# Loading Q of a grouped-query attention kernel: sixteen DMA transposes, or eight plain loads and transposes on TensorE

## Chip, cores and metric

The kernel runs on one core of a Trainium2 chip. The metric is the device time of one execution in microseconds (us), as the median of several runs. A profiled execution ("the profile", "the trace") gives spans; its span is 1.8 us shorter than the measured time where the record gives both for one execution.

## The reference

```python
B, Hq, Hkv, Sq, Sk, D = 16, 32, 8, 16, 2048, 128        # all bf16
k = jnp.repeat(k, 4, axis=1); v = jnp.repeat(v, 4, axis=1)
scores = jnp.einsum("bhqd,bhkd->bhqk", q, k) * D ** -0.5
out    = jnp.einsum("bhqk,bhkd->bhqd", jax.nn.softmax(scores, axis=-1), v)
```

The four query heads of a key head have 4 x 16 = 64 query rows, so there are 128 groups of 64 rows, and the kernel takes them two at a time: 64 **pairs** of 128 rows. K and V are 64 MiB each; Q and the output are 2 MiB each. Each pair needs 2 MiB of K and V.

## The kernel before

For each pair the work is: transpose both groups' K on TensorE into PSUM and evict it (KT), multiply Q by it (S), take the row maximum on VectorE (`max`), exponentiate on ScalarE (`exp`), transpose the probabilities on TensorE and evict them (PT), multiply by V (PV), normalise (`norm`) and store. Q lies transposed in SBUF, as `QT[d, row]`, and is the stationary operand of S.

A 128x1024 half tile of KT or PT passes through one of only three staging banks of PSUM. VectorE or ScalarE evicts it. A bank must have been evicted before the third half tile after it can be transposed.

The order of the operations on each engine is fixed when the kernel is built. A generator, `build_schedule`, plays a list-scheduling model with assumed durations and DMA rates and writes down the order in which things start. Its times are assumptions, but the order it chose is then binding: in the traces before the change TensorE ran its 5,632 instructions in exactly the generated order.

```python
_DUR = {"KT_load": 0.46, "PT_load": 0.46, "S": 0.75, "PV": 1.02, ...
        ("act", "kte"): 1.07, ("act", "pte"): 1.07, ("act", "exp"): 2.08, ..., "Q": 3.3}
_SIZE = {"K": 0.5, "V": 0.5, "Q": 0.25 * 1.45, "ST": 0.03125 * 1.45}
QCH = 512            # rows of Q per load: one load serves four pairs
...
sched = build_schedule(NP, pairs_per_qch)
pe_prog, dve_prog, act_prog, sp_prog = sched["pe"], sched["dve"], sched["act"], sched["sp"]
...
def issue_q(c):      # SyncE: one of sixteen DMA transposes of 512 rows
    sp.dma_start_transpose(QT[:, qch * c:qch * (c + 1)], qf[qch * c:qch * (c + 1), :]).then_inc(sem_q[c], 16)
...
# TensorE, transposes of K: one staging bank per half
pe.wait_ge(sem_k[s], 16 * (g // NBK + 1))
for ld in lds:
    wait_bank_free(ld)
    for t in range(8):
        ins = pe.transpose(stage_ap(ld["bank"], t), Kn[s][:, 8 * ld["half"] + t, :], ident[:, :])
    ins.then_inc(sem_stage, 1)
...
# TensorE, score product: QT is the stationary operand
ins = pe.matmul(S_ps[64 * gg:64 * (gg + 1), 512 * c:512 * (c + 1)],
                QT[:, 128 * p + 64 * gg:128 * p + 64 * (gg + 1)],
                kt[:, gg, 4 * c:4 * (c + 1), :], start=True, stop=True)
...
# ScalarE, eviction (VectorE has the same with tensor_copy)
act.wait_ge(sem_stage, ld["u"] + 1)
act.activation(evac_dst(ld), stage_bank_ap(ld["bank"]), ACT.Copy).then_inc(sem_ev["act"], 1)
```

SyncE issues all DMAs in order: K two tiles per pair, V three pairs later, the store seven pairs later. There are 12 buffers for K and 16 for V.

Of the kernel before, what the change touches and what calls it, by code (L numbers as in the profile page):

```python
# [16 lines left out]
NSTAGE = 3  # L17
DV = 3
DSTORE = 7
QCH = 512  # L20
QLEAD = 6


_DUR = {
    "KT_load": 0.46, "PT_load": 0.46, "S": 0.75, "PV": 1.02,
    ("dve", "kte"): 0.63, ("dve", "pte"): 0.63, ("dve", "max"): 2.30, ("dve", "recip"): 0.17, ("dve", "norm"): 0.36,
    ("act", "kte"): 1.07, ("act", "pte"): 1.07, ("act", "exp"): 2.08, ("act", "norm"): 0.46,
    "K": 0.65, "V": 0.65, "ST": 0.65, "Q": 3.3,
}
_LAT = 0.12  # L30
_LAT_SAME = 0.04
# [1 line left out]
_BW = 0.371  # L33
_BW_SLOW = 0.364
_RING_MB = 5.2
_SIZE = {"K": 0.5, "V": 0.5, "Q": 0.25 * 1.45, "ST": 0.03125 * 1.45}
_T0 = 7.0


# [20 lines left out]
def build_schedule(NP, qch_pairs, nbk=NBK, nbv=NBV, nbo=NBO, nkt=NKT, npt=NPT, nstage=NSTAGE, opts=None):  # L60
# [6 lines left out]
    def t(key):  # L67
        return done.get(key, INF)

    pe_left = []  # L70
    for p in range(NP):
        pe_left += [("KT", p, 0), ("KT", p, 1), ("S", p), ("PT", p), ("PV", p)]
    x_left = []
    for p in range(NP):
        x_left += [("kte", p, gg, h) for gg in range(2) for h in range(2)]
        x_left += [("pte", p, h) for h in range(2)]
        x_left += [("max", p), ("recip", p), ("exp", p), ("norm", p)]
# [12 lines left out]
    def eng_options(op):  # L90
        k = op[0]
        if k in ("max", "recip"):
            return ("dve",)
        if k == "exp":
            return ("act",)
        if k == "kte":
            return opts["kte_engs"]
        if k == "pte":
            return opts["pte_engs"]
        return opts["norm_engs"]  # L100

    def ready_pe(op):
        kind = op[0]
        r = []
        if kind == "KT":
            p, gg = op[1], op[2]
            r.append(t(("dma", "K", 2 * p + gg)))
            if p >= nkt and ("S", p - nkt) not in pe_sched:
                return INF
            u0 = next_u[0]  # L110
            for h in range(2):
                if u0 + h >= nstage:
                    r.append(t(("evac", u0 + h - nstage)))
        elif kind == "S":
            p = op[1]
            r.append(t(("dma", "Q", p // qch_pairs)))
            for gg in range(2):
                for hh in range(2):
                    key = ("KT", p, gg, hh)
                    if key not in load_u:  # L120
                        return INF
                    r.append(t(("evac", load_u[key])))
            if p >= 1:
                r.append(t(("max", p - 1)))
        elif kind == "PT":
            p = op[1]
            r.append(t(("exp", p)))
            if p >= npt and ("PV", p - npt) not in pe_sched:
                return INF
            u0 = next_u[0]  # L130
            for h in range(2):
                if u0 + h >= nstage:
                    r.append(t(("evac", u0 + h - nstage)))
        elif kind == "PV":
            p = op[1]
            for hh in range(2):
                key = ("PT", p, None, hh)
                if key not in load_u:
                    return INF
                r.append(t(("evac", load_u[key])))  # L140
            for gg in range(2):
                r.append(t(("dma", "V", 2 * p + gg)))
            if p >= 1:
                r.append(t(("norm", p - 1)))
        return max(r) if r else 0.0

    def ready_x(op):
        kind = op[0]
        r = []
        if kind == "kte":  # L150
            key = ("KT", op[1], op[2], op[3])
            if key not in load_u:
                return INF
            r.append(t(("load", load_u[key])))
        elif kind == "pte":
            key = ("PT", op[1], None, op[2])
            if key not in load_u:
                return INF
            r.append(t(("load", load_u[key])))
        elif kind == "max":  # L160
            p = op[1]
            r.append(t(("S", p)))
            if p >= 2:
                r.append(t(("exp", p - 2)))
        elif kind == "recip":
            r.append(t(("exp", op[1])))
        elif kind == "exp":
            p = op[1]
            r.append(t(("max", p)))
            if p >= 2:  # L170
                r.append(t(("PT", p - 2)))
        elif kind == "norm":
            p = op[1]
            r += [t(("PV", p)), t(("recip", p))]
            if p >= nbo:
                r.append(t(("dma", "ST", p - nbo)))
        return max(r) if r else 0.0
# [10 lines left out]
    def ready_sp(op):  # L188
        kind, x = op
        r = [ring_ok_time(_SIZE[kind])]  # L190
        if kind == "K":
            if x >= nbk:
                r.append(t(("KT", (x - nbk) // 2, (x - nbk) % 2)))
        elif kind == "V":
            if x >= nbv:
                r.append(t(("PV", (x - nbv) // 2)))
        elif kind == "ST":
            r.append(t(("norm", x)))
        return max(r) if r else 0.0

    KIND_PRIO = {"S": 0, "max": 0, "exp": 0, "PT": 1, "pte": 1, "PV": 2, "recip": 2, "norm": 2, "KT": 3, "kte": 3}

    while pe_left or x_left or sp_left:
        best = None
# [7 lines left out]
        for op in pe_left:  # L212
            rd = ready_pe(op)
            if rd == INF:
                continue
            st = max(free["pe"] + _LAT_SAME, rd + _LAT)
            cand = ((round(st, 3), op[1], KIND_PRIO[op[0]]), st, "pe", op)
            if best is None or cand[0] < best[0]:
                best = cand
            seen += 1  # L220
            if seen > 12:
                break
        seen = 0
        for op in x_left:
# [7 lines left out]
                engs = (fin[0][1],)  # L232
            for eng in engs:
                st = max(free[eng] + _LAT_SAME, rd + _LAT)
                cand = ((round(st, 3), op[1], KIND_PRIO[op[0]]), st, eng, op)
                if best is None or cand[0] < best[0]:
                    best = cand
            seen += 1
# [17 lines left out]
        elif eng == "pe":  # L256
            pe_left.remove(op)
            pe_sched.add(op)
            if kind in ("KT", "PT"):
                en = st  # L260
                for h in range(2):
                    uu = next_u[0]
# [11 lines left out]
        else:  # L274
            x_left.remove(op)
            en = st + DUR[(eng, kind)]
            if kind == "kte":
                done[("evac", load_u[("KT", op[1], op[2], op[3])])] = en
            elif kind == "pte":
                done[("evac", load_u[("PT", op[1], None, op[2])])] = en  # L280
            else:
                done[(kind, op[1])] = en
# [7 lines left out]
def bass_standalone__gqa_softmax__sampling_kernel(  # L290
# [27 lines left out]
    ident = sb("ident", [128, 128], BF16)  # L318
    iota_t = sb("iota_t", [128, 128], I32)
    QT = sb("QT", [128, NROWS], BF16)  # L320
    Kn = [sb(f"Kn{i}", [128, J, 128], BF16) for i in range(NBK)]
    Vb = [sb(f"Vb{i}", [128, J, 128], BF16) for i in range(NBV)]
    KT = [sb(f"KT{i}", [128, 2, J, 128], BF16) for i in range(NKT)]
# [29 lines left out]
    loads = []  # L353
    kt_loads = {}
    pt_loads = {}
    for op in pe_prog:
        if op[0] == "KT":
            _, p, gg = op
            for h in range(2):
                ld = dict(kind="KT", pair=p, gg=gg, half=h, u=len(loads), eng=None, eidx=None)  # L360
# [9 lines left out]
                pt_loads[(p, h)] = ld  # L370

    def op_load(op):
        if op[0] == "kte":
            return kt_loads[(op[1], op[2], op[3])]
        if op[0] == "pte":
            return pt_loads[(op[1], op[2])]
        return None
# [49 lines left out]
    with nc.Block() as block:  # L427
# [7 lines left out]
        @block.sync  # L435
        def _(sp):
            def issue_q(c):
                sp.dma_start_transpose(QT[:, qch * c:qch * (c + 1)], qf[qch * c:qch * (c + 1), :]).then_inc(sem_q[c], 16)

            def issue_k(g):  # L440
                s = g % NBK
# [38 lines left out]
        def _(pe):  # L480
# [6 lines left out]
                    pe.wait_ge(sem_ev[prev["eng"]], prev["eidx"])  # L487

            for op in pe_prog:
                if op[0] == "KT":  # L490
                    _, p, gg = op
                    lds = [kt_loads[(p, gg, h)] for h in range(2)]
                    g = grp(p, gg)
# [8 lines left out]
                        ins.then_inc(sem_stage, 1)  # L502
                elif op[0] == "S":
                    _, p = op
                    pe.wait_ge(sem_q[(128 * p) // qch], 16)
                    for sm, n in evac_waits([kt_loads[(p, gg, h)] for gg in range(2) for h in range(2)]):
                        pe.wait_ge(sm, n)
                    if p >= 1:
                        pe.wait_ge(sem_max, p)
# [21 lines left out]
                elif op[0] == "PV":  # L531
# [18 lines left out]
                            )  # L550
                    ins.then_inc(sem_pv, 1)

        def evac_dst(ld):
            p, h = ld["pair"], ld["half"]
            if ld["kind"] == "KT":
                return KT[p % NKT][:, ld["gg"], 8 * h:8 * (h + 1), :]
            return PT[p % NPT][:, 8 * h:8 * (h + 1), :]

        @block.vector
        def _(dve):  # L560
            for op in dve_prog:
                ld = op_load(op)
                if ld is not None:
                    dve.wait_ge(sem_stage, ld["u"] + 1)
                    dve.tensor_copy(evac_dst(ld), stage_bank_ap(ld["bank"])).then_inc(sem_ev["dve"], 1)  # L565
                elif op[0] == "recip":
                    p = op[1]
                    dve.wait_ge(sem_exp, p + 1)
# [21 lines left out]
        def _(act):  # L590
            for op in act_prog:
                ld = op_load(op)
                if ld is not None:
                    act.wait_ge(sem_stage, ld["u"] + 1)
                    act.activation(evac_dst(ld), stage_bank_ap(ld["bank"]), ACT.Copy).then_inc(sem_ev["act"], 1)  # L595
                elif op[0] == "exp":
                    kk = op[1]
                    act.wait_ge(sem_max, kk + 1)
# [43 lines left out]
```

## Time and profile before

| | before |
|---|---|
| time, median of 3 runs | 373.71 us |
| span of the profiled execution | 370.2 us |
| TensorE, VectorE, ScalarE busy | 331.0, 323.0, 261.9 us |
| common distance between PV products of successive pairs | 5.29 us |
| mean distance over four pairs, with one Q load | 5.52 us |

These are lines of the page of the kernel before. The first has each engine's busy time. Then come busy tenths in 40 slices of the span for TensorE and DMA, with the granted TensorE clock between them; the q1 line of the DMA queues, with packets, megabytes and the share of the 16 engines' time; and the engine shares of the chain that ended last. After that come one group of instructions (count, then busy us and mean ns of one, then idle time before them and what ended most of it) and the Q line of the DMA issues (the last number is us from issue to landing).

```profile
PE 331.0 (89%) x5632; PEld 260.2 (70%) x5632; DVE 323.0 (87%) x500; ACT 261.9 (71%) x269; POOL 1.0 (0%) x6
...
PE   4698998998998989999898999989999898999995
...
PEclk9899999999999999999999999999999999999999
DMA  7999999999999999999999999999999999999993
...
q1 hardware_dynamic: 54784, 138.43, 102.3%
...
PE 68%; ACT 21%; issue 4%; DMA 4%; DVE 3%
...
L595 ACT ACTIVATE PT<-ST_ps 128x1024 bf16<-128x1024 bf16 x59 | 57.2, 1021 | 42.2 <-PE ST_ps L529 42.2
...
QT<-in_q_dram SPq DMA_TRANSPOSE x16, 12.3
```

TensorE and VectorE are nearly full in every slice, and so is DMA. The full DMA row does not mean that DMA is the limit: the chain is TensorE and ScalarE, with 4% of DMA. An eviction of 128x1024 takes ScalarE 1.02 us when it reads and writes in order.

Which of the two holds the kernel is seen from who waits for whom. These are lines of the waits view (who <- for whom: us in total, times, longest):

```profile
...
PE ST_ps L501 <- ACT KT L595: 8.1, 27, 0.4
PE ST_ps L501 <- ACT PT L595: 5.3, 24, 0.2
PE ST_ps L501 <- DMA Kn<-in_k_dram: 4.5, 1, 4.5
...
PE O_ps L544 <- DMA Vb<-in_v_dram: 1.0, 1, 1.0
```

TensorE waited for a K load once, at the very start, and for a V load once. It waited for ScalarE's evictions again and again, 0.2 to 0.4 us each. SyncE's own waits include this one, in which a store waits for the pair to be normalised, and the loads queue up behind it:

```profile
...
SPq L462 <- DVE O L586: 14.1, 11, 5.1
```

This is one normal pair in the timeline of TensorE (start us, duration us, engine, line, operation, tiles, count, and in brackets the idle time before it and who ended it):

```profile
...
166.02 1.08 PE L544 MATMUL O_ps<-Vb,PT 128*64 128x128 bf16 x32
167.03 1.07 PE L501 MATMUL ST_ps<-ident,Kn 128*128 128x128 bf16 x16
168.03 1.05 PE L513 MATMUL S_ps<-KT,QT 128*64 128x512 bf16 x8
169.02 1.07 PE L529 MATMUL ST_ps<-ident,P 128*128 128x128 bf16 x16
169.92 0.61 PE L501 MATMUL ST_ps<-ident,Kn 128*128 128x128 bf16 x8
170.75 0.62 PE L501 MATMUL ST_ps<-ident,Kn 128*128 128x128 bf16 x8 [0.22 <-ACT PT L595]
171.31 0.41 PE L544 MATMUL O_ps<-Vb,PT 128*64 128x128 bf16 x7
```

The two PV products (the first and last line) start 5.29 us apart, with one gap of 0.22 us, waiting for ScalarE to free a staging bank. The PT transposed at 169.02 is not the one the PV at 171.31 uses: in this order PV runs on probabilities that were transposed and evicted a pair earlier.

### The profile page before, as it was taken

Reading aid. Unit: us, or ns where it says so; the run is one execution under the profiler, and the core shown is the slowest. Engines: PE = TensorE matmul, PEld = TensorE weight load, DVE = VectorE, ACT = ScalarE, POOL = GpSimd, SP = SyncE. Lnnn points to the kernel's source line nnn. Section 1 sums busy time; section 2 is a strip of 40 time slices with the busy share of each in tenths; the row PEclk is TensorE's granted clock in tenths of the full one; section 3 lists DMA queues with packets and bytes.
Section 4 is the critical chain, followed back from the end, with each engine's and each line's share of the span. In section 5 each row is a group of like instructions: output and inputs, shape, how many; then the busy total and the mean of one; then the engine's idle time right before and its main releaser. Section 6 shows DMA issues by size and latency. Waiting matters only on the chain.

```text
span 370.2 us, 13021 instructions
## 1 busy us (share of the span) xinstructions
PE 331.0 (89%) x5632; PEld 260.2 (70%) x5632; DVE 323.0 (87%) x500; ACT 261.9 (71%) x269; POOL 1.0 (0%) x6
## 2 busy tenths in 40 slices
PE   4698998998998989999898999989999898999995
PEld 3576876776776767677776777777777676776764
DVE  2589998998998989899898998989899897999984
ACT  1267766895666885867878676795867778679593
POOL 1000000000000000000000000000000000000000
PEclk9899999999999999999999999999999999999999
DMA  7999999999999999999999999999999999999993
GB/s 262 375 408 341 408 352 405 405 345 407 352 407 410 342 408 350 406 409 347 410 347 408 400 350 413 348 410 370 380 410 346 408 350 399 409 410 410 406 410 112
DMA packets 54840, 139.26 MB, mean 376 GB/s; under 512 B 22016, under 2 KB 22016, under 8 KB 54784
## 3 DMA queue, kind: packets, MB, share of 16 engines
q1 hardware_dynamic: 54784, 138.43, 102.3%
q8 instruction: 45, 0.74, 0.8%
q14 instruction: 11, 0.09, 0.1%
HBM read 134.22 MB, written 2.10 MB: 368 GB/s over the span
## 4 chain that ended last, share of the span: by engine, by line
PE 68%; ACT 21%; issue 4%; DMA 4%; DVE 3%
PE ST_ps L501 26%; PE S_ps L513 17%; PE O_ps L544 14%; PE ST_ps L529 11%; ACT KT L595 11%; ACT PT L595 8%; DMA Vb<-in_v_dram 3%; DVE Sneg L575 2%; ACT P L601 1%; DMA Kn<-in_k_dram 1%; DVE KT L565 1%; DVE PT L565 0%; DVE O L586 0%; DVE rrec L569 0%
## 5 line engine op out<-in xcount | busy, mean ns | idle before, releaser
L575 DVE TENSOR_SCALAR_CACHE_REDUCE Sneg<-S_ps 128x2048 f32<-128x2048 f32 x64 | 146.7, 2292 | 18.6 <-PE S_ps L513 15.1
L501 PE MATMUL ST_ps<-ident,Kn 128*128 128x128 bf16 x2048 | 143.6, 223 | 18.6 <-ACT KT L595 8.1
L501 PEld LDWEIGHTS ST_ps<-ident,Kn 128*128 128x128 bf16 x2048 | 119.6, 99 | 45.1 <-issue 26.7
L601 ACT ACTIVATE P<-Sneg,nbias 128x2048 bf16<-128x2048 f32 x64 | 128.3, 2005 | 11.5 <-DVE Sneg L575 11.5
L565 DVE COPY KT<-ST_ps 128x1024 bf16<-128x1024 bf16 x177 | 116.3, 683 | 9.8 <-PE ST_ps L501 7.6
L595 ACT ACTIVATE KT<-ST_ps 128x1024 bf16<-128x1024 bf16 x79 | 77.6, 1022 | 48.4 <-PE ST_ps L501 48.3
L595 ACT ACTIVATE PT<-ST_ps 128x1024 bf16<-128x1024 bf16 x59 | 57.2, 1021 | 42.2 <-PE ST_ps L529 42.2
L529 PE MATMUL ST_ps<-ident,P 128*128 128x128 bf16 x1024 | 71.6, 220 | 7.5 <-ACT KT L595 3.8
L529 PEld LDWEIGHTS ST_ps<-ident,P 128*128 128x128 bf16 x1024 | 58.2, 98 | 25.1 <-issue 11.4
L513 PE MATMUL S_ps<-KT,QT 128*64 128x512 bf16 x512 | 68.4, 388 | 6.6 <-ACT KT L595 4.4
L544 PE MATMUL O_ps<-Vb,PT 128*64 128x128 bf16 x2048 | 69.6, 220 | 4.2 <-issue 1.4
L544 PEld LDWEIGHTS O_ps<-Vb,PT 128*64 128x64 bf16 x2048 | 59.1, 110 | 11.1 <-issue 2.5
L565 DVE COPY PT<-ST_ps 128x1024 bf16<-128x1024 bf16 x69 | 44.3, 683 | 3.4 <-PE ST_ps L529 3.2
L513 PEld LDWEIGHTS S_ps<-KT,QT 128*64 128x64 bf16 x512 | 25.3, 109 | 26.3 <-issue 9.9
L586 DVE TENSOR_SCALAR O<-O_ps,rrec 128x128 bf16<-128x128 f32 x62 | 21.5, 346 | 9.1 <-PE O_ps L544 9.1
L569 DVE RECIPROCAL rrec<-rowsum 128x1 f32<-128x1 f32 x64 | 10.2, 159 | 4.3 <-ACT P L601 4.1
L601 ACT ACTIVATION_READ_ACCUMULATOR P<-Sneg,nbias 128x1 f32 x64 | 12.9, 202 | 0.0
L575 DVE DVE_READ_ACCUMULATOR Sneg<-S_ps 128x1 f32 x64 | 5.3, 83 | 0.0
L601 ACT ACT_TABLE_LOAD x1 | 1.3, 1283 | 0.7 <-PEq L627 0.7
L612 ACT ACTIVATE O<-O_ps,rrec 128x128 bf16<-128x128 f32 x2 | 0.7, 368 | 0.4 <-PE O_ps L544 0.4
L433 POOL TENSOR_SCALAR ident<-iota_t 128x128 bf16<-128x128 int32 x1 | 0.5, 536 | 0.1
L431 POOL IOTA iota_t<- 128x128 int32 x1 | 0.2, 235 | 0.4 <-POOLq L627 0.4
(4 smaller groups left out, 0.4 us busy)
## 6 DMA issues: line engine op xcount, KB each, us to landing
Kn<-in_k_dram SPq DMA_DIRECT2D x128, 512.0 KB, 12.9
Vb<-in_v_dram SPq DMA_DIRECT2D x128, 512.0 KB, 12.9
out_dram<-O SPq DMA_DIRECT2D x64, 32.0 KB, 12.6
QT<-in_q_dram SPq DMA_TRANSPOSE x16, 12.3
```

What stands on the lines that cost most here:

```text
L433: gp.tensor_scalar(ident[:, :], iota_t[:, :], 0.0, None, op0=ALU.is_equal).then_inc(sem_id, 1)
L501: ins = pe.transpose(stage_ap(ld["bank"], t), Kn[s][:, j, :], ident[:, :])
L513: ins = pe.matmul(S_ps[64 * gg:64 * (gg + 1), 512 * c:512 * (c + 1)], QT[:, 128 * p + 64 * gg:128 * p + 64 * (gg + 1)], kt[:, gg, 4 * c:4 ...
L529: ins = pe.transpose(stage_ap(ld["bank"], t), P[p % 2][:, 128 * j:128 * (j + 1)], ident[:, :])
L544: ins = pe.matmul(O_ps[64 * gg:64 * (gg + 1), 0:128], pt[:, j, 64 * gg:64 * (gg + 1)], Vb[g % NBV][:, j, :], start=(j == 0), stop=(j == J ...
L565: dve.tensor_copy(evac_dst(ld), stage_bank_ap(ld["bank"])).then_inc(sem_ev["dve"], 1)
L569: dve.reciprocal(rrec[:, p:p + 1], rowsum[:, p:p + 1]).then_inc(sem_rec, 1)
L575: dve.tensor_scalar(Sneg[kk % 2][:, :], S_ps[:, :], -scale, None, op0=ALU.mult, op1=ALU.min, accum_out=nbias[:, kk:kk + 1],).then_inc(sem_ ...
L586: dve.tensor_scalar(Osb[s_][:, :], O_ps[:, 0:128], rrec[:, p:p + 1], None, op0=ALU.mult).then_inc(sem_nm["dve"], 1)
L595: act.activation(evac_dst(ld), stage_bank_ap(ld["bank"]), ACT.Copy).then_inc(sem_ev["act"], 1)
L601: act.activation(P[kk % 2][:, :], Sneg[kk % 2][:, :], ACT.Exp, bias=nbias[:, kk:kk + 1], scale=-1.0, accum_out=rowsum[:, kk:kk + 1],).then ...
L612: act.activation(Osb[s_][:, :], O_ps[:, 0:128], ACT.Copy, scale=rrec[:, p:p + 1]).then_inc(sem_nm["act"], 1)
```

## The change

Its intent is to take the DMA transposes, which cost the DMA engines much time for little data (about 2.1 us for 128 KB, as the prediction reads from the trace), out of the stream of K and V loads. Q is loaded in eight plain loads of 1024 rows, eight consecutive rows in each partition (2 KB runs). Each such load is transposed on TensorE, eight 128x128 transposes into one staging bank. ScalarE evicts the bank to `QT`. Since partition `a` holds rows `8a ... 8a+7`, transposed tile `i` has rows `8a+i`. The eviction puts the columns in order by writing with a step of eight elements. The generator gets the new operations, priced like the other evictions. The core of the diff:

```diff
-QCH = 512
+QCH = 1024
-    ..., "Q": 3.3,
+    "QT_load": 0.46, ..., ("dve", "qte"): 1.2, ..., ("act", "qte"): 1.07, ..., "Q": 0.65,
-_SIZE = {..., "Q": 0.25 * 1.45, ...}
+_SIZE = {..., "Q": 0.25, ...}
+        if p % qch_pairs == 0:
+            pe_left.append(("QT", p // qch_pairs))     # and ("qte", ...) for ScalarE, in the generator
 ...
-                sp.dma_start_transpose(QT[:, qch * c:qch * (c + 1)], qf[qch * c:qch * (c + 1), :]).then_inc(sem_q[c], 16)
+                if c >= 2:
+                    sp.wait_ge(sem_stage, qt_loads[c - 2]["u"] + 1)
+                src = qf[qch * c:qch * (c + 1), :].rearrange("(a i) d -> a i d", a=128)
+                sp.dma_start(Qn[c % 2][:, :, :], src).then_inc(sem_q[c], 16)
 ...
+                if op[0] == "QT":
+                    pe.wait_ge(sem_q[op[1]], 16)
+                    wait_bank_free(ld)
+                    for i in range(qch // 128):
+                        ins = pe.transpose(stage_ap(ld["bank"], i), Qn[op[1] % 2][:, i, :], ident[:, :])
+                    ins.then_inc(sem_stage, 1)
 ...
+        def evac_src(ld):
+            src = stage_bank_ap(ld["bank"])
+            return src.rearrange("d (i a) -> d i a", a=128) if ld["kind"] == "QT" else src
 ...
+            if ld["kind"] == "QT":
+                return QT[:, qch * p:qch * (p + 1)].rearrange("d (a i) -> d i a", a=128)
-                    act.activation(evac_dst(ld), stage_bank_ap(ld["bank"]), ACT.Copy).then_inc(sem_ev["act"], 1)
+                    act.activation(evac_dst(ld), evac_src(ld), ACT.Copy).then_inc(sem_ev["act"], 1)
```

## The prediction

> **What bounds the kernel now.** By the page, TensorE is 89% busy, VectorE 87%, ScalarE 71%, and DMA is busy in every slice (376 GB/s mean). Two limits run side by side.
>
> - DMA. By the landings in the trace, V tiles of successive pairs land 5.16 us apart where no Q transpose lies between. Four pairs with one Q transpose take 22.75 us, not 4 x 5.16 = 20.6: one 128 KB DMA transpose costs the stream 2.1 us (about 60 GB/s). [...]
> - Compute. The timeline shows a fixed order. Most pairs take 5.29 us between starts of their PV products: 5.06 us of back-to-back TensorE work and a 0.22 us wait for ScalarE to evict a staging bank. Around each Q load one pair has another order and takes about 6.2 us, so four pairs take 22.1 us. In the waits view TensorE waits for ScalarE again and again, for V only once (1.0 us, at 310 us), for K only at the start.
>
> So V lands ahead of its use: 7 us early on, 0.6 us less every four pairs, 0.2 us at pair 51. DMA nearly catches the kernel, but the compute order holds it.
>
> **What the change does.**
>
> - Removes sixteen transposes: 34 us of DMA stream, and over 4 us each on SP's queue[...].
> - Adds eight plain 256 KB loads, 0.64 us each at 409 GB/s. DMA then needs 42 us per eight pairs, 5.24 a pair, less than compute.
> - Adds 64 TensorE transposes: 8 take 0.5 us (half of a 16-tile K load of 1.0 us), 4 us in all. Adds eight ScalarE evictions of 128x1024, 1.02 us each like the present ones; the strided write may add a little. Each borrows one of three staging banks.
> - Regenerates the static order, with a shorter Q load, once per eight pairs instead of four.
>
> **How much is on the critical path.** Some 29 us of DMA goes, but DMA is only 4% of the chain. To be gained: the V wait (1 us) and slow pairs in the order, 0.95 us each, fifteen of them. To be paid: 0.5 us TensorE and 0.2-0.7 us of bank wait per Q tile, perhaps still one slow pair per Q tile. Over the 5.29 pace, eight pairs lose 1.9 us before, and about 1.0-2.0 after; I take 1.5. So 8 x 0.4 = 3 us gained, and 1 us for the V wait; start and end even: 4 us of 374.
>
> **Prediction: 369.5 us, range 362.5 to 374.5. Faster by over 2%: 0.26; within 2%: 0.70; slower by over 2%: 0.04.**
>
> **What would show it.** SP waits longer for buffers; q1's share of DMA time is below 100%; V lands 5 us or more before use throughout, with no TensorE wait for V. TensorE busy about 335 us, ScalarE about 270. PV starts 5.29 us apart in most pairs, one longer interval per eight; TensorE's waits still on ScalarE's evictions.
>
> **What would make it wrong.** If the new order keeps no slow pairs and Q's transposes fill TensorE's idle time, the gain reaches 10 us or more. If the shorter DMA changes the normal order, the 5.29 us pace itself moves, either way. If the strided eviction is far slower than 1 us and delays exp, or TensorE waits for banks oftener, the gain is gone. If the first score product waits long for Q's eviction, the start loses 1-2 us.

The sum: 8 x 0.4 = 3 us and 1 us for the V wait, 4 us in all. The "over 4 us each on SP's queue" were 4.5 us at the median in the trace before (1.2 to 7.1 us for the sixteen transposes).

## More of the kernel before

All timed runs here of more than one round are of the fast state. Three runs were single looks, of state unknown, and are marked.

## The result, and the profile after

The change made the kernel slower: 423.10 us (420.92 to 425.07, 4 runs) against 373.63 us (4 runs), ratio 1.134, 95% interval 1.129 to 1.138. Ratios here are the mean time of one kernel's fast runs over that of the other's of the same rounds, so they are not quite the ratio of the quoted medians. The prediction was 369.5 us, in a range of 362.5 to 374.5.

The page of the changed kernel, the lines that answer to those above (here the chain has its second line too, with shares by line):

```profile
PE 346.9 (82%) x5696; PEld 270.1 (64%) x5696; DVE 334.9 (79%) x513; ACT 287.7 (68%) x264; POOL 1.0 (0%) x6
...
PE   4779996999859998599949999499994999999994
...
PEclk9899997999969999899987999989999999999999
DMA  8999999999976999879993999958999489998500
...
q1 hardware_dynamic: 47232, 138.43, 86.4%
...
PE 70%; ACT 26%; issue 2%; DMA 1%; ACTq 0%; DVE 0%
PE ST_ps L548 24%; PE S_ps L560 16%; PE ST_ps L576 15%; PE O_ps L591 14%; ACT PT L648 13%; ACT QT L648 9%; ACT P L654 3%; ACT KT L648 1%; DMA Kn<-in_k_dram 1%; PE ST_ps L535 1%; ACTq L464 0%; DVE PT L618 0%; DVE O L639 0%
...
L648 ACT ACTIVATE PT<-ST_ps 128x1024 bf16<-128x1024 bf16 x107 | 103.7, 1021 | 89.2 <-PE ST_ps L576 89.2
...
L648 ACT ACTIVATE QT<-ST_ps 128x1024 bf16<-128x1024 bf16 x8 | 37.6, 4698 | 6.4 <-PE ST_ps L535 6.4
```

The DMA side did what was intended: the DMA row now has holes. q1's share went from 102.3% to 86.4%, but much of that fall is the longer span: in e5 below, whose span of 373.1 us is close to that of the kernel before, the share is 96.4%. But TensorE's busy share fell from 89% to 82%. Its row shows slices of 4, 5 or 6 tenths at regular distances, and at most of them the granted clock falls to between 6 and 8 tenths. The last line names the culprit: eight evictions of QT take 4,698 ns each, where an eviction of PT of the same 128x1024 takes 1,021 ns. On the chain they are 9% of the span.

The waits view of the changed kernel:

```profile
...
PE ST_ps L576 <- ACT QT L648: 27.0, 6, 4.6
...
PE O_ps L591 <- ACT PT L648: 20.7, 52, 1.6
...
PE ST_ps L548 <- ACT PT L648: 10.8, 48, 0.3
```

Two new waits stand here. TensorE waited 27.0 us for QT's eviction, up to 4.6 us at a time. And PV waited for PT's eviction 52 times, 20.7 us in all, a wait that is not in the list before. SyncE's wait for a pair to be normalised shows which way the pressure runs now. Loads wait for compute:

```profile
...
SPq L502 <- DVE O L639: 228.9, 62, 9.4
```

It was 14.1 us before. By the landing times in the trace, V now lands 6 to 25 us ahead of its use.

One of the stalls in the timeline of the changed kernel:

```profile
...
111.00 1.05 PE L560 MATMUL S_ps<-KT,QT 128*64 128x512 bf16 x8
...
116.45 4.69 ACT L648 ACTIVATE QT<-ST_ps 128x1024 bf16<-128x1024 bf16 x1
...
121.29 1.87 PE L576 MATMUL ST_ps<-ident,P 128*128 128x128 bf16 x16 [4.57 <-ACT QT L648]
...
123.08 1.92 PE L560 MATMUL S_ps<-KT,QT 128*64 128x512 bf16 x8
...
124.93 1.89 PE L548 MATMUL ST_ps<-ident,Kn 128*128 128x128 bf16 x16
```

ScalarE starts the eviction of QT at 116.45 and is busy with it until 121.14. The next `exp` and PT wait behind it in ScalarE's program, and TensorE stands still for 4.57 us. The eight score matmuls after it take 1.92 us, in place of the 1.05 us of the same eight at 111.00. The clock record of the trace has TensorE at half clock from 120.15 to 126.98 us. The other tiles show the same: seven of the eight stop TensorE for 3.92 to 4.57 us, and within 1.2 us of the end of each of these stops a half-clock stretch of 3.4 or 6.8 us begins, 34.1 us together. At the eighth stop, of 1.71 us, there is none. How long a stop must be is not shown: in the kernel before, whose only half-clock stretch within the span is from 16.38 to 19.80 us, a stop of 2.70 us came before it.

A normal pair also became slower. This is TensorE around one PV:

```profile
...
102.42 0.62 PE L548 MATMUL ST_ps<-ident,Kn 128*128 128x128 bf16 x8 [0.22 <-ACT PT L648]
103.33 1.08 PE L591 MATMUL O_ps<-Vb,PT 128*64 128x128 bf16 x32 [0.29 <-ACT PT L648]
104.35 1.07 PE L548 MATMUL ST_ps<-ident,Kn 128*128 128x128 bf16 x16
```

PV now waits 0.29 us for ScalarE's eviction of its own PT, besides the 0.22 us of the bank wait. PV products are 5.65 us apart, not 5.29. A listing of the generator's two orders shows why (a K half is the K tile of one of the pair's two groups): before, TensorE's program runs PT(29), a K half, PV(28); after, it runs PT(29), a K half, PV(29). The regenerated order runs the software pipeline one pair tighter. Which of the changed entries of the generator made it choose so was not examined.

So the theory after reading the traces has two parts. **A**: the eviction's scattered write to SBUF costs 3.7 us more per tile, in front of everything ScalarE has to do, and the half clock behind it. **B**: the regenerated order costs 0.36 us per pair. The rivals are that the stalls come from where the Q tile stands in the order, whatever its eviction costs; and that the order is harmless.

### The profile page after: what moved, and what is told of

Same layout as the page of the kernel before. It is cut to its first block, busy times and chain, and to the rows that moved or that the text cites. A ratio compares the mean times of both kernels' runs of the same rounds, so it can differ in the third digit from the quotient of the medians.

```text
span 421.9 us, 13111 instructions
## 1 busy us (share of the span) xinstructions
PE 346.9 (82%) x5696; PEld 270.1 (64%) x5696; DVE 334.9 (79%) x513; ACT 287.7 (68%) x264; POOL 1.0 (0%) x6
## 2 busy tenths in 40 slices
DMA packets 47288, 139.27 MB, mean 330 GB/s; under 512 B 13440, under 2 KB 13440, under 8 KB 47232
## 3 DMA queue, kind: packets, MB, share of 16 engines
q1 hardware_dynamic: 47232, 138.43, 86.4%
## 4 chain that ended last, share of the span: by engine, by line
PE 70%; ACT 26%; issue 2%; DMA 1%; ACTq 0%; DVE 0%
PE ST_ps L548 24%; PE S_ps L560 16%; PE ST_ps L576 15%; PE O_ps L591 14%; ACT PT L648 13%; ACT QT L648 9%; ACT P L654 3%; ACT KT L648 1%; DMA Kn<-in_k_dram 1%; PE ST_ps L535 1%; ACTq L464 0%; DVE PT L618 0%; DVE O L639 0%
## 5 line engine op out<-in xcount | busy, mean ns | idle before, releaser
L618 DVE COPY KT<-ST_ps 128x1024 bf16<-128x1024 bf16 x236 | 155.0, 683 | 18.3 <-PE ST_ps L548 18.0
L648 ACT ACTIVATE PT<-ST_ps 128x1024 bf16<-128x1024 bf16 x107 | 103.7, 1021 | 89.2 <-PE ST_ps L576 89.2
L548 PE MATMUL ST_ps<-ident,Kn 128*128 128x128 bf16 x2048 | 149.9, 226 | 17.6 <-ACT PT L648 10.8
L548 PEld LDWEIGHTS ST_ps<-ident,Kn 128*128 128x128 bf16 x2048 | 123.1, 101 | 38.1 <-ACT PT L648 18.5
L591 PE MATMUL O_ps<-Vb,PT 128*64 128x128 bf16 x2048 | 70.4, 222 | 21.6 <-ACT PT L648 20.7
L560 PE MATMUL S_ps<-KT,QT 128*64 128x512 bf16 x512 | 71.8, 404 | 4.3 <-ACT QT L648 3.9
L648 ACT ACTIVATE QT<-ST_ps 128x1024 bf16<-128x1024 bf16 x8 | 37.6, 4698 | 6.4 <-PE ST_ps L535 6.4
L648 ACT ACTIVATE KT<-ST_ps 128x1024 bf16<-128x1024 bf16 x20 | 19.5, 1021 | 32.1 <-PE ST_ps L548 32.1
L639 DVE TENSOR_SCALAR O<-O_ps,rrec 128x128 bf16<-128x128 f32 x64 | 22.4, 351 | 21.7 <-PE O_ps L591 21.7
L618 DVE COPY PT<-ST_ps 128x1024 bf16<-128x1024 bf16 x21 | 14.1, 689 | 27.8 <-PE ST_ps L576 27.6
L535 PE MATMUL ST_ps<-ident,Qn 128*128 128x128 bf16 x64 | 4.9, 219 | 0.0
L535 PEld LDWEIGHTS ST_ps<-ident,Qn 128*128 128x128 bf16 x64 | 3.9, 98 | 0.0
```

The source lines that it names most:

```text
L535: ins = pe.transpose(stage_ap(ld["bank"], i), Qn[op[1] % 2][:, i, :], ident[:, :])
L548: ins = pe.transpose(stage_ap(ld["bank"], t), Kn[s][:, j, :], ident[:, :])
L591: ins = pe.matmul(O_ps[64 * gg:64 * (gg + 1), 0:128], pt[:, j, 64 * gg:64 * (gg + 1)], Vb[g % NBV][:, j, :], start=(j == 0), stop=(j == J ...
L618: dve.tensor_copy(evac_dst(ld), evac_src(ld)).then_inc(sem_ev["dve"], 1)
L639: dve.tensor_scalar(Osb[s_][:, :], O_ps[:, 0:128], rrec[:, p:p + 1], None, op0=ALU.mult).then_inc(sem_nm["dve"], 1)
L648: act.activation(evac_dst(ld), evac_src(ld), ACT.Copy).then_inc(sem_ev["act"], 1)
```

## The experiments

Twelve kernels ran, and every one gave correct results. Each change is shown against the changed kernel unless said otherwise.

### Two by two: eviction and order

`e1_row_tiles` deals the rows to partitions so that a transposed tile holds 128 consecutive rows. The eviction then needs no permutation; the price is DMA runs of 256 B.

```diff
-    src = qf[...].rearrange("(a i) d -> a i d", a=128)
+    src = qf[...].rearrange("(i a) d -> a i d", a=128)
-    return src.rearrange("d (i a) -> d i a", a=128) if ld["kind"] == "QT" else src
+    return src
-    return QT[:, qch * p:qch * (p + 1)].rearrange("d (a i) -> d i a", a=128)
+    return QT[:, qch * p:qch * (p + 1)]
```

> The changed kernel with the order untouched; only the rows of Q are dealt to partitions so that each transposed tile holds 128 consecutive rows, and ScalarE evicts it contiguously (DMA runs of 256 B instead of 2 KB). Theory A (the eviction's scattered write is the main cost): QT's eviction falls from 4.69 us to about 1.02 us, no TensorE gap over 3 us and no half-clock stretches remain after the start, and the time falls by 8 x (3.7 to 4.6) = 30 to 37 us, to 386-394 us. It stays above the kernel before, since the order still paces a pair at 5.65 us. Rival B (the stalls come from where the order puts the Q tile, whatever its eviction costs): the time stays above 412 us. Rival C (the order is harmless, only the eviction hurts): the time falls to 370 us or less.

`e5_old_order_contig` is e1 with the generator of the kernel before, unchanged, and the eight Q tiles put into its order:

```diff
-    sched = build_schedule(NP, pairs_per_qch)
+    sched = old_order(NP)   # old generator; QT(c) before PV(8c-10) on TensorE, its eviction at
+                            # the matching place on ScalarE; DMA order as in the changed kernel
```

> As e1_row_tiles, but the engines run the order of the kernel before, with the eight Q tiles put in (before the PV product of pair 8c-10). Theory (the new order costs 0.36 us a pair because PV of a pair follows the eviction of its own PT, and the old order has slow pairs at every fourth): normal pairs 5.29 us apart instead of 5.65, slow pairs remain, and the time is 373-380 us, some 8-15 us below e1_row_tiles. Rival (order is indifferent): equal to e1_row_tiles within 3 us.

`e6_old_order_strided` has the same `old_order` but the change's own load and eviction.

> The fourth corner: the old order with Q tiles put in, and the change's own load and scattered eviction. If eviction and order add up: e5_old_order_contig plus the same 30-37 us, so 405-415 us. If the stalls need the new order: within 10 us of e5_old_order_contig.

| time, us (before: 373.30) | new order | old order, Q tiles put in |
|---|---|---|
| scattered eviction, 4.7 us | 423.10 (the change; its own rounds) | 408.84 (e6, ratio 1.095) |
| contiguous eviction, 1.02 us | 385.37 (e1, ratio 1.033) | 375.10 (e5, ratio 1.006) |

Both parts hold. The 385.37 us of e1 lie below what rival B asks and above what rival C asks, so both fall; they are 0.6 us below the range of theory A. Making the eviction contiguous takes 37.7 us off in the new order and 33.7 us in the old one. The old order takes 14.3 or 10.3 us off. In e1 QT's evictions take 1,023 ns, and the granted clock is 0.998 where it was 0.958. This is their group on e1's page:

```profile
...
L648 ACT ACTIVATE QT<-ST_ps 128x1024 bf16<-128x1024 bf16 x8 | 8.2, 1023 | 7.0 <-PE ST_ps L535 7.0
```

The eviction and the half clock behind it went together. The two pages, with the same TensorE instructions in the same order, differ by 38.3 us of span: TensorE is idle 25.6 us longer in the changed kernel (75.0 against 49.4) and busy 12.7 us longer (346.9 against 334.2). An estimate from this is that about a third of the loss is the half clock. No run takes the half clock away alone, so that share is argued and not shown.

In e5 normal pairs are 5.29 us apart again, and per eight pairs there are three slow ones: two of 6.2 us, as before, and one of 6.3 us with the Q tile. So even with the eviction that the prediction had assumed, and with the pace it had assumed, the kernel gains nothing.

### What makes the eviction slow

`e4_stride_ladder` (one look, state unknown) uses 8, 8, 4, 4, 2, 2, 1 and 1 rows per run in the eight loads. The same 128x1024 eviction thus writes with a step of 16, 8, 4 and 2 bytes.

```diff
+RUN = [8, 8, 4, 4, 2, 2, 1, 1]
-    src = qf[...].rearrange("(a i) d -> a i d", a=128)
+    src = qf[...].rearrange("(b a i) d -> a b i d", a=128, i=RUN[c])
-    return src.rearrange("d (i a) -> d i a", a=128) if ...
+    return src.rearrange("d (b i a) -> d b i a", a=128, i=RUN[ld["pair"]]) if ...
-    return QT[...].rearrange("d (a i) -> d i a", a=128)
+    return QT[...].rearrange("d (b a i) -> d b i a", a=128, i=RUN[p])
```

> The changed kernel with 8, 8, 4, 4, 2, 2, 1 and 1 rows per partition run in chunks 0 to 7, so the eviction's write step is 16, 16, 8, 8, 4, 4, 2 and 2 bytes, same 128x1024 each. [...] If every non-contiguous write of 2-byte elements is slow, it takes about 4.7 us at 16, 8 and 4 bytes, and 1.0 us only at 2. [...] it falls in between, about halving with each halving of the step. Time 395 to 410 us.

One eviction of each step, from ScalarE's timeline of that run (start us, duration us), in the order 16, 8, 4 and 2 bytes:

```profile
...
20.24 4.72 ACT L649 ACTIVATE QT<-ST_ps 128x1024 bf16<-128x1024 bf16 x1
...
65.06 2.44 ACT L649 ACTIVATE QT<-ST_ps 128x1024 bf16<-128x1024 bf16 x1
...
201.03 1.31 ACT L649 ACTIVATE QT<-ST_ps 128x1024 bf16<-128x1024 bf16 x1
...
294.40 1.02 ACT L649 ACTIVATE QT<-ST_ps 128x1024 bf16<-128x1024 bf16 x1
```

The time halves with the step until 4 bytes. From 16 to 8 bytes it falls by 2.28 us, and from 8 to 4 bytes by 1.13 us. An estimate from these: both give 0.28 us per byte of step, on top of some 0.2 us. At 2 bytes that would be about 0.74 us, but 1.02 us were measured, so something else sets the time there. Why the write's time follows its step is not shown, and a step of more than 16 bytes was not run. The time came to 392.82 us, 2 us below its expected range.

`e2_strided_read` (one look, state unknown) walks the same elements in the other order. The write is contiguous, and the read of PSUM steps 256 bytes. The 2 KB runs of the load stay.

```diff
-    return src.rearrange("d (i a) -> d i a", a=128) if ld["kind"] == "QT" else src
+    return src.rearrange("d (i a) -> d a i", a=128) if ld["kind"] == "QT" else src
-    return QT[:, qch * p:qch * (p + 1)].rearrange("d (a i) -> d i a", a=128)
+    return QT[:, qch * p:qch * (p + 1)].rearrange("d (a i) -> d a i", a=128)
```

> The changed kernel with its load and order; the eviction walks the same elements in the other order, so that the write to SBUF is contiguous and the read of PSUM steps 256 bytes. If only scattered writes to SBUF are slow: eviction 1.02 us and a time of 384-394 us, as e1_row_tiles. If ScalarE is slow on any scattered access: eviction over 2 us and a time above 395 us.

Its QT group on the page:

```profile
...
L648 ACT ACTIVATE QT<-ST_ps 128x1024 bf16<-128x1024 bf16 x8 | 8.2, 1024 | 7.1 <-PE ST_ps L535 7.1
```

This scattered read of PSUM cost ScalarE nothing (1,024 ns against 1,021), and the time is 384.01 us. The order of two letters in two access patterns is worth some 39 us against the change.

`e11_dve_evicts` (one look, state unknown; its base is e9 below) lets VectorE do the scattered eviction.

```diff
-    act.insert(act.index(("exp", q + 2)), ("qte", c))
+    dve.insert(dve.index(("kte", q + 4, 0, 0)), ("qte", c))     # and the first one likewise
```

> e9_periodic_strided with VectorE in ScalarE's place for Q's scattered eviction. [...] about 4.5-4.8 us here too. If it is ScalarE's own trouble: 1.0-1.4 us (VectorE's contiguous 128x1024 copy takes 0.68 us[...]).

```profile
...
L639 DVE COPY KT<-ST_ps 128x1024 bf16<-128x1024 bf16 x256 | 162.1, 691 | 8.6 <-PE ST_ps L569 7.2
...
L639 DVE COPY QT<-ST_ps 128x1024 bf16<-128x1024 bf16 x8 | 37.4, 4677 | 0.3 <-PE ST_ps L556 0.3
```

VectorE takes 4,677 ns, though its contiguous copy of this size takes 691 ns in this run (683 ns in the kernel before). So the price is that of the scattered write to SBUF and not of ScalarE. The time was 393.02 us.

### What the order costs

`e13_one_pair_later` takes e1 and writes the normal pattern of the new order by hand, for all pairs, with K, S and PT one pair further ahead of PV. VectorE evicts all of KT and ScalarE all of PT, as in that order's normal pairs. Two things come with it: the irregular pairs of e1 go (there ScalarE evicts 20 half tiles of KT and VectorE 21 of PT), and each Q tile stands before PV(8c-10).

```diff
-    sched = build_schedule(NP, pairs_per_qch)
+    # per pair t: PV(t) KT(t+4) half 0, S(t+3), PT(t+2), KT(t+4) half 1
+    #   (the new order's normal pairs: PV(t) KT(t+3) half 0, S(t+2), PT(t+1), KT(t+3) half 1)
+    (pe_prog, dve_prog, act_prog), sp_prog = periodic_order(NP, True), sp_program(NP, pairs_per_qch)
```

> e1_row_tiles with only the software pipeline loosened: the normal pattern of the changed kernel (PV, first K half, S, PT, second K half; VectorE evicts all KT, ScalarE all PT) is kept for all pairs, but K, S and PT run one pair further ahead of PV, so that a PV product never follows the eviction of its own PT. Theory (this is why the new order paces a pair at 5.65 us): the 0.29 us wait of PV for ScalarE goes from every pair, normal pairs take 5.25-5.32 us, and the time falls from 385 to 362-370 us. Rival (the slower pace comes from ScalarE having both PT halves to evict, whatever the distance): 5.6 us a pair, 380 us or more.

The time is 363.72 us (before in the same rounds: 373.75; ratio 0.974, interval 0.967 to 0.981, which at 2% is unclear), 21.7 us below e1. Normal pairs are 5.29 us apart. PV's wait for ScalarE's eviction of PT, in the waits view of e13:

```profile
...
PE O_ps L612 <- ACT PT L669: 0.6, 1, 0.6
```

The 20.7 us of the changed kernel (e1 has 20.7 us too) became 0.6 us, with ScalarE evicting every PT tile. So theory B holds and its rival falls: the distance between PT and its PV made the slower pace. A part of the 21.7 us comes from the regular pattern, which has one slow pair per eight (6.28 us, the one with the Q tile).

### Was there anything to gain from the DMA side?

In the kernel before, a few early pairs ran with another pattern, two K halves in a row, and pairs 4 and 6 took 5.05 us each. (The first expectation below says pairs 3 to 6, which is too much: pair 3 took 5.20 and pair 5 took 5.82 us.) The next kernels use that pattern for all pairs, with K half a pair further ahead.

```python
def periodic_order(NP, with_qt=True):              # cut: rolling out, putting in the Q tiles
    pe_t  = [("PV", 0), ("KT", 4, 0), ("KT", 4, 1), ("S", 3), ("PT", 2)]     # op of pair t + lag
    dve_t = [("norm", 0), ("recip", 1), ("kte", 4, 0, 0), ("kte", 4, 0, 1),
             ("kte", 4, 1, 0), ("kte", 4, 1, 1), ("max", 3)]
    act_t = [("exp", 2), ("pte", 2, 0), ("pte", 2, 1)]
    ...   # QT(c) before PV(8c-10), its eviction before exp of pair 8c-8
```

`e7_periodic_contig` is e1 with this order. `e8_periodic_dmat` is the kernel before, with its sixteen DMA transposes, in this order. `e9_periodic_strided` is the changed kernel, with its scattered eviction, in this order.

> Plain loads of Q with contiguous eviction, as e1_row_tiles, and one hand-written pattern for all pairs: PV(t), both K halves of t+4, S(t+3), PT(t+2); VectorE evicts all of KT, ScalarE all of PT. The kernel before runs this pattern in its pairs 3 to 6, at 5.05 us a pair. Theory (DMA transposes were a second limit just behind the compute order, so their removal pays once the order is better): TensorE runs at 5.05-5.15 us, the DMA stream at 5.24 us a pair becomes the pace, and the time is 350-358 us, a gain of 15-23 us over the kernel before. Rival (the compute side cannot go below 5.29 us a pair over a long stretch): 365 us or more.

> The same pattern with the sixteen DMA transposes of the kernel before. Theory: now the DMA stream, 22.75 us per four pairs, is the limit; TensorE waits for V or K at every Q load, V's lead goes to zero early, and the time is 368-374 us: the better order alone gains almost nothing. Rival (DMA transposes were never a limit, only the order was): as fast as e7_periodic_contig within 4 us.

> The same pattern with the change's own load and scattered eviction of 4.69 us. If the eviction's cost sits on ScalarE in the way of exp and PT whatever the order: e7_periodic_contig plus 8 x (3.7 to 4.6) = 30-37 us. If a looser pipeline absorbs part of it (ScalarE has over 1.5 us of slack a pair): plus 10-25 us.

| in the periodic order | time, us (before: 373.31) | ratio to before |
|---|---|---|
| e8: DMA transposes | 375.79 | 1.005 |
| e9: plain load, scattered eviction | 388.51 | 1.042 |
| e7: plain load, contiguous eviction | 360.36 | 0.965 |

The DMA transposes were a real second limit, hidden behind the compute order. With them the faster order gains nothing (e8 came out 1.8 us above its expected range), and TensorE waits for K and V all along. The waits view of e8:

```profile
...
PE ST_ps L522 <- DMA Kn<-in_k_dram: 23.6, 28, 4.4
...
PE O_ps L565 <- DMA Vb<-in_v_dram: 4.3, 6, 1.2
```

Between Q loads the pairs of e8 are about 5.2 us apart, and 6.9 us at each Q load, which is the rhythm in which the trace lets K and V land. Without them the same order runs 15.4 us faster. e7 itself missed its expectation (350-358 us) by 2.4 us. Its normal pairs take 4.96 us, but the waits view shows this:

```profile
...
PE ST_ps L556 <- DMA Qn<-in_q_dram: 11.0, 7, 2.5
...
PE ST_ps L569 <- DMA Kn<-in_k_dram: 5.0, 3, 4.5
```

e9 fell between its two alternatives: the scattered eviction costs 28.2 us here, against 37.7 in the tight order, so a looser pipeline absorbs only a little of it. The slack of over 1.5 us a pair that its expectation counts on is not there: `exp` (2.03 us), the read of its sum (0.20) and two evictions of PT (1.02 each) leave ScalarE some 0.7 us of a normal pair's 4.96 us.

`e10_periodic_late_qt` puts the Q tile five pairs later and uses the load and the eviction of e2. `e12_late_qt_row_tiles` has only the later place.

```diff
-            q = max(8 * c - 10, 0)
+            q = max(8 * c - 5, 0)
```

> e7_periodic_contig with two changes: the Q tile is transposed five pairs later (before PV(8c-5), in place of PV(8c-10)), and Q keeps its 2 KB runs, with the scattered access on the PSUM read as in e2_strided_read. In e7 TensorE waited 11.0 us for Q to land, seven times, because the tile stood too early in its order. Theory: that wait goes, 9-11 us are gained, and the time is 348-353 us. Rival (those waits hid a DMA limit that comes back as waits for K or V): 356 us or more.

> As e10_periodic_late_qt, but with e7's load in 256 B runs and contiguous eviction, so that only the place of the Q tile differs from e7. If the place is what mattered: within 2 us of e10. If the 256 B runs cost DMA time that now counts (e1 and e2 differed by 1.4 us, one run of the second): 2-5 us above e10.

Against 372.81 us for the kernel before, e10 takes 357.34 us (ratio 0.958, interval 0.957 to 0.959), the fastest kernel, and e12 takes 359.97 us (ratio 0.965, as e7). The rival was right. The wait for Q went and came back as waits for K and V:

```profile
...
PE ST_ps L569 <- DMA Kn<-in_k_dram: 9.4, 15, 4.4
...
PE O_ps L612 <- DMA Vb<-in_v_dram: 2.9, 6, 1.0
```

The place of the Q tile gained nothing, and the 2 KB runs gained the 2.6 us. Three rows of the 40 slices on e10's page, TensorE, DMA and bandwidth, show the limit that is left:

```profile
PE   4899999999999998999999899999999999989965
DMA  7999999999999999999999999999999999999960
GB/s 289 416 407 408 408 408 410 411 410 410 408 410 410 411 412 408 409 412 411 408 412 409 410 410 409 410 411 408 411 405 410 411 411 412 411 405 393 397 237 13
```

The DMA stream runs at 405 to 416 GB/s in nearly every slice between the first and the last few. An estimate: 139.27 MB (the page's total) at 410 GB/s are 340 us of the 355.5 us span.

## Why the prediction was wrong

- **The eviction's size.** The step that failed reads: "Adds eight ScalarE evictions of 128x1024, 1.02 us each like the present ones; the strided write may add a little." It measured 4.70 us. This term alone, with the half clock that followed it, is 37.7 us (e1 against the change). The prediction did list a strided eviction "far slower than 1 us" among what could go wrong, but did not size it, and its range left no room for it. The durations that it took from the trace were of a different access pattern. Nothing in the trace before showed a scattered write.
- **The pace.** "Over the 5.29 pace, eight pairs lose 1.9 us before, and about 1.0-2.0 after" took the pace as given. The regenerated order ran at 5.65 us, because PV follows the eviction of its own PT. Loosening that by one pair, in a regular pattern, gave 21.7 us back (e13). This too stood under what would make the prediction wrong, "either way".
- **The half clock** was not thought of. In the trace of the change it came with each of the seven standstills of TensorE of 3.92 to 4.57 us, 3.4 or 6.8 us of it each time; what that costs was not isolated.
- **What was right.** DMA was not the limit before; q1's share fell below 100%, helped by the longer span; V lands over 5 us ahead; TensorE never waits for V; SyncE waits longer for compute. The 34 us of transposes lay off the path, as it said (e5 gains nothing from their removal), and e8 against e7 shows that they were a limit waiting behind the first.
- **TensorE busy about 335 us, ScalarE about 270** became 346.9 and 287.7. With the eviction mended (e1) they are 334.2 and 258.6.
- **The gain of 4 us.** Even with the eviction and the pace that the prediction assumed, e5 is 0.6% slower than before: two slow pairs per eight stayed, and the Q tiles came on top with a third.

## What to carry to other kernels

Before moving work to another engine, price it by its access pattern and not by its element count: a permutation belongs on the side of the copy where it is free (here the read of PSUM, 1.02 us) and not on the write to SBUF (4.70 us). When an order is generated from assumed costs, a changed cost changes the whole order; compare the normal stretch of the two timelines first, and look for a product that follows directly on the eviction it needs. And here the DMA transposes, a load on a nearly full DMA stream, paid nothing when removed (e5, 375.10 us against 373.30) until the compute order in front of them was made faster (e7, 360.36 us against the 375.79 of e8): do both, and test them in a two-by-two.
